# A recurrent attention and a gated network in one planned kernel: decay factors in PSUM, in-place weight conversion, a fourth group buffer, product diagonals for the early groups, and a second DMA queue

## The chip, the cores and the metric

One core of one Trainium2 chip. The metric is the device time of one execution in microseconds, the median of three runs.

## The reference

Two stages, one after the other. The first is a linear recurrence per batch and head (4 batches, 8 heads, 768 tokens, head size 48); the second a gated network on the joined heads (384 columns, 1024 hidden).

```python
for t in range(S):
    cur = einsum('bhd,bhe->bhde', u * k[t], v[t])
    y[t] = einsum('bhd,bhde->bhe', r[t], state + cur)
    state = w * state + einsum('bhd,bhe->bhde', k[t], v[t])

h = maximum(x @ w_in, 0)                      # x: y with its heads joined
conv = sum(conv_w[k] * h shifted by k-1 tokens for k in 0..2)
out = (h * sigmoid(conv)) @ w_out
```

## The kernel before

**Recurrence.** 64 tokens form a chunk, two chunks a group of 128 tokens, six groups a batch; 24 groups in all. Eight heads are four pairs, one head of a pair on partitions 0 to 47, the other on 64 to 111. `load(g)` brings a group into one of `NBUF` buffers: `KR` (k and r with the head dimension on partitions) and `TOK` (k, r and v with tokens on partitions). `prep(g)` scales KR by the decay factors `TKR` (powers of w and their inverses) on VectorE, and TOK's k by `TH`. It also makes the diagonal of the score matrix: r times k, times u, summed over the head dimension (`QQ`), and spread along a diagonal (`SC`, from `eye` and QQ). `visit(g, av, su)` is TensorE's work for a group: `su` makes the next group's scores (`SP`) and state sums (`UP`), `av` this group's output (`AV`). After it, VectorE copies the masked scores into SC (`msk`), the states are updated (`M` decays, `SA` adds; tiles `MM` and `SS`), and `AV` is split into a high and a low part in `XT`. Six small move-copies (SBUF to SBUF DMAs, class `mv`) then bring the fourth pair's rows of XT beside the other three pairs.

**Network.** The tokens of all batches are cut into nine units (the first batch in three of some 256 tokens, the others in two of some 384). For each unit and each of eight hidden blocks, `first(i)` runs nine matmuls into a PSUM bank `HP` (of `NH`), then ReLU, the middle tap (`T1`) on ScalarE, two taps (`T2`, L509) on VectorE into `CV`, the sigmoid into `SG`, the gate product (`GG`, L513) on VectorE, which is the last reader of the HP bank, and a split of the product into two parts in one of 13 `GG` buffers. `second(u, k)` takes three matmuls per hidden block into `PO`; after eight blocks ScalarE copies `PO` to `OS` and a DMA writes it out. "A nine" is nine matmuls of either layer.

**Weights.** They arrive as 64-bit words. `convert` stages a piece in one of `NST` buffers `ST`, makes two 32-bit parts in `CC` (ScalarE) and `TT` (VectorE: a shift, L368, then a combine, L370), and splits the result into a high part (ScalarE cast) and a low part (a subtraction). There are eight pieces of `w_in` and six wider ones of `w_out`.

**Order.** Nothing is scheduled by hand. Every operation is entered in `Plan` with its engines, a duration, and the tiles that it reads and writes. `Plan.order` is a list scheduler: by due times and durations it picks what comes next on each engine, and for operations marked "any" also the engine. It also inserts filler matmuls on `wz` before the first network matmul. The durations are the numbers in `dve`, `pool`, `act` and at each `op`; each engine then keeps the order so found, and the chip's semaphores do the waiting. L272 is the helper `tt` that records all two-input products, so its instructions are told apart by tile. All DMAs are issued from SP (L275).

Of the kernel before, what the change touches and what calls it, by code (L numbers as in the profile page):

```python
# [42 lines left out]
OFF = {"wz": 50.0, "wcz": 60.0}  # L43


class Plan:
# [6 lines left out]
    def __init__(self):  # L53
        self.ops = []
        self.last_w, self.last_r = {}, {}
        self.port = []

    def op(self, eng, dur, rd, wr, fn, cls="", x=0.0, port=False, mode=0):
# [19 lines left out]
        self.port.append(port)  # L78
        return n

    def late(self):
        ops, n = self.ops, len(self.ops)
        late = [1e6] * n
        t = T0
        for i, (dur, x, *_) in enumerate(ops):
            if "pe" in dur and x:
                late[i] = t
                t += dur["pe"]
        for i in reversed(range(n)):
            for j in ops[i][2]:  # L90
                d, x = ops[j][:2]
                m = min(d.values()) + LAT if "sp" not in d else d["sp"] + x + 1.5
                late[j] = min(late[j], late[i] - m)
        return [t - OFF.get(o[4], 0.0) for t, o in zip(late, ops)]

    def order(self):
# [19 lines left out]
        mode = 0  # L116
        todo = n
        while todo:
            best = None
            for e in self.ENG:  # L120
                av, f = avail[e], free[e]
                if e == "pool":
                    c = []
                    for i in av:
                        if len(ops[i][0]) > 1:
                            s = max(free["dve"], ready[i])
                            bl = sum(ops[k][0]["dve"] for k in avail["dve"] if late[k] < late[i] and ready[k] <= s)
                            if max(f, ready[i]) + ops[i][0]["pool"] > s + bl + ops[i][0]["dve"] + PB:
                                continue
                        c.append(i)  # L130
                    av = c
# [53 lines left out]
            elif e == "sp":  # L185
# [3 lines left out]
                lanes.append(done)  # L189
                free[e] = max(free[e], lanes.pop(0))  # L190
# [23 lines left out]
def rwkv_ffn_kernel(tc, krd, krt, vt, wd, ut, w_in, conv_w, w_out, out):  # L214
# [4 lines left out]
    with ExitStack() as ctx:  # L219
# [18 lines left out]
        OS = sb([128, U], F32, "OS", 2)  # L238
        ST = sb([128, 1024], I32, "ST", NST)
        CC, TT = sb([128, 512], F32, "CC", NST), sb([128, 512], I32, "TT", NST)  # L240
# [5 lines left out]
        DN, PW = sb([112, NP, C], F32, "DN"), sb([112, NP, 96], F32, "PW")  # L246
        TKR = sb([112, 2, NP, C], F32, "TKR")
        TK, TR = TKR[:, 0], TKR[:, 1]
        TH = sb([128, NP, D], F32, "TH")
        wi = [sb([128, 3, DF], F32R, f"wi{i}") for i in range(2)]  # L250
# [16 lines left out]

        def tt(eng, n, rd, wr, cls="", psum=0, **kw):
            d = {"dve": dve(n, psum=psum), "pool": pool(n)}
# [4 lines left out]
        def dma(rd, wr, dst, src, dur=0.5, x=0.1, cls=""):  # L274
            op("sp", dur, rd, wr, lambda e: SP.dma_start(dst, src), cls, x)  # L275
# [5 lines left out]
        def warm(e):  # L281
            for _ in range(NW):
                PE.matmul(PO, wz[:, :128], wz, start=True, stop=True)
        op("dve", 0.274, [], ["wz"], lambda e: V.memset(wz, 0.0))
        op("pe", 0.2134 * NW, ["wz"], ["PO"], warm, "warm", 512 * NW)
# [5 lines left out]
        for i, k in enumerate(KR):  # L291
            op("dve", 0.5, [], [n for n in kr(i) if n[2] == 0], lambda e, k=k: V.memset(k[32:64], 0.0), "KRz")

        def load(g):
# [3 lines left out]
            dma([], [("tK", i), ("tR", i)], TOK[i][:, 0:2], krt[g], 0.45, 1.05, "ldT")  # L298
            for x in range(2):
                xs = slice(x * C, (x + 1) * C)  # L300
                dma([], [("tV", i, x)], TOK[i][xs, 2], vt[g, xs, x], 0.45, 0.3, "ldV")

        load(0)
        dma([], ["uu"], uu, ut, 0.45, 0.4, "ldU")
# [50 lines left out]

        ncv = [0]

        def convert(srcs, n, dst, view, keys, cls):
            i = ncv[0] % NST
            ncv[0] += 1  # L360
            st, cc, t = ST[i][:, :2 * n], CC[i][:, :n], TT[i][:, :n]
            s2 = st.rearrange("q (n two) -> q n two", two=2)
            sk = [("ST", i, k) for k in range(len(srcs))]
            for k, (to, src) in zip(sk, srcs):
                dma([], [k], to(st), src, 0.45, n / 352.0 / len(srcs), "wdma")
            op("act", act(n, 1), sk, [("CC", i)], lambda e: A.activation(
                cc, s2[:, :, 1].bitcast(F32), AF.Prelu, scale=2.0 ** -111, alpha=2.0 ** 32))
            op("dve", dve(n, 2) + 0.1, sk, [("TT", i)], lambda e: V.tensor_scalar(  # L368
                out=t, in0=s2[:, :, 0], scalar1=29, scalar2=None, op0=ALU.logical_shift_right), port=True)
            op("dve", dve(n) + 0.06, [("CC", i)], [("TT", i)], lambda e: V.scalar_tensor_tensor(  # L370
                out=t, in0=cc.bitcast(I32), scalar=3, in1=t, op0=ALU.logical_shift_left, op1=ALU.bitwise_or), port=True)
            tf = view(t.bitcast(F32))
            if len(dst) == 1:
                op("act", act(n, 1), [("TT", i)], keys, lambda e: A.activation(dst[0], tf, AF.Copy, scale=1.0 / WS))
                return
            op("act", act(n, 1), [("TT", i)], [keys[0]], lambda e: A.copy(dst[0], tf), cls + "h")
# [17 lines left out]
        def prep(g):  # L394
# [3 lines left out]
            tkr = TKR.rearrange("q a p t -> q (a p) t").unsqueeze(2).broadcast_to([112, 2 * NP, 2, C])  # L398
            if g < 2:
                for h, n in ((0, "KK"), (1, "RR")):  # L400
                    hs = slice(4 * h, 4 * h + 4)
                    tt("dve", 512, ["TK1", "TK2"] if h == 0 else ["TR1", "TR2"], [k for k in kr(i) if k[0] == n], "KR", out=kr_[:, hs], in0=kr_[:, hs], in1=tkr[:, hs], op=ALU.mult)
            else:
                tt("dve", 1024, ["TK1", "TK2", "TR1", "TR2"], kr(i), "KR", out=kr_, in0=kr_, in1=tkr, op=ALU.mult)
            tt("any", 384, [("tK", i)], [("tR", i)], "KRT", out=r_t, in0=r_t, in1=k_t, op=ALU.mult)
            tt("any", 384, ["TH"], [("tK", i)], "KS", out=k_t, in0=k_t, in1=TH.unsqueeze(2).broadcast_to([128, NP, 2, D]), op=ALU.mult)
            tt("any", 384, ["uu"], [("tR", i)], "KRU", out=r_t, in0=r_t, in1=uu.unsqueeze(2).broadcast_to([128, NP, 2, D]), op=ALU.mult)
# [3 lines left out]
            tt("any", 512, [("QQ", g % 2), "eye"], [("SC", g % 2)], "dg", out=SC[g % 2].rearrange("q p c t -> q (p c) t"),  # L411
               in0=eye.unsqueeze(1).broadcast_to([128, 2 * NP, C]), in1=q.unsqueeze(2).broadcast_to([128, 2 * NP, C]), op=ALU.mult)
# [6 lines left out]
        def visit(g, av, su):  # L419
# [9 lines left out]
            if su:  # L429
                rd += kr(j) + [("tK", j), ("tV", j, 0), ("tV", j, 1)]  # L430
                wr += ["SUs", "SUu"]

            def mm(e):
                for c in range(2):
                    for p in range(NP):
# [4 lines left out]
                        for x in range(2):  # L440
                            if su:
                                PE.matmul(SP_[xs[x], p, c], KK[j][rows[x], p, t], RR[j][rows[x], p, t], start=True, stop=True)  # L442
# [206 lines left out]
```

## Time and profile before

| | |
|---|---|
| median of 3 runs | 331.6 us (330.52 to 337.47) |
| profiled execution | 332.88 us, span 331.2 us |
| busy: TensorE, VectorE | 296.4 us (90%), 265.3 us (80%) |
| busy: ScalarE, GpSimd | 168.9 us (51%), 185.5 us (56%) |
| mean granted TensorE clock | 0.948 |
| DMA | 37.78 MB, 114 GB/s on average |

The profile names PE (TensorE matmul), PEld (its weight loads), DVE (VectorE), ACT (ScalarE), POOL (GpSimd) and SP (the engine that issues the DMAs). A group of instructions reads: line, engine, operation, output<-inputs, shapes, count | busy us, mean ns | idle time of the engine just before them and what ended it. A row of the chain of waits reads: start us, duration us, what. "SPq" is SP issuing a DMA.

### The profile page before, as it was taken

The page shows a single profiled execution, that of the slowest core. Times are in us where ns is not written, and L with a number is a line of the kernel's source. Part 1 is how long each engine was busy: PE and PEld are TensorE (multiplying, and loading weights), DVE is VectorE, ACT ScalarE, POOL GpSimd, SP SyncE. Part 2 cuts the span into 40 slices and gives each one's busy share as a digit, 9 for nine tenths or more (in the row PEclk, how much of TensorE's full clock was granted, in tenths as well). Part 3 has the DMA queues.
Part 4 walks back from the last instruction along what each step waited for, and adds up shares of the span by engine and source line. Part 5 has one row for each costly group of instructions (what it writes and reads, how often), then busy time and mean ns, then how long its engine had stood idle before and what let it go on. Part 6 is the DMA issues. An engine that isn't in the chain of part 4 may idle for free.

```text
span 331.2 us, 10563 instructions
## 1 busy us (share of the span) xinstructions
PE 296.4 (90%) x4371; PEld 277.0 (84%) x4371; DVE 265.3 (80%) x439; ACT 168.9 (51%) x380; POOL 185.5 (56%) x201
## 2 busy tenths in 40 slices
PE   6888668795979968998699999999999999999995
PEld 1677657694969967998699999999998999999995
DVE  7897779897988967997597879998999986556630
ACT  2222475664554464376354653676464756567631
POOL 4657668694956844546956746894477632131000
PEclk9797786789899997999799999999999999999999
DMA  6956775745344353455336425443474111000011
GB/s 177 251 160 185 208 226 157 180 132 132 97 115 114 109 149 90 91 131 139 88 101 173 117 81 150 132 113 81 103 179 107 35 34 41 12 26 25 26 48 49
DMA packets 25952, 37.78 MB, mean 114 GB/s; under 512 B 5168, under 2 KB 19504, under 8 KB 25904
## 3 DMA queue, kind: packets, MB, share of 16 engines
q1 hardware_dynamic: 25904, 37.11, 42.1%
q8 instruction: 34, 0.56, 0.7%
q14 instruction: 14, 0.11, 0.1%
HBM read 30.01 MB, written 4.72 MB: 105 GB/s over the span
## 4 chain that ended last, share of the span: by engine, by line
PE 50%; DVE 20%; DMA 10%; issue 6%; POOL 6%; ACT 5%; SPq 2%; DVEq 0%; ACTq 0%; POOLq 0%
PE HP L500 20%; PE PO L532 19%; DMA ST<-in_w_out_dram 6%; DVE CV L509 4%; DVE KR L272 3%; PE SP L442 3%; PE HP L532 3%; POOL TOK L272 2%; DVE GG L272 2%; PE AV L452 2%; POOL GG L272 2%; SPq L275 2%; PE AV L445 2%; DMA TOK<-in_krt_dram 2%; DVE TT L370 1%
## 5 line engine op out<-in xcount | busy, mean ns | idle before, releaser
L500 PE MATMUL HP<-XT,wi 128*128 128x384 f32 (+4 forms) x648 | 123.3, 339 | 15.6 <-DVE SG L513 10.2
L500 PEld LDWEIGHTS HP<-XT,wi 128*128 128x128 f32 x648 | 110.9, 204 | 18.7 <-DVE SG L513 11.8
L532 PE MATMUL PO<-GG,wo 128*128 128x382 f32 (+4 forms) x600 | 110.7, 327 | 8.6 <-POOL GG L272 2.9
L532 PEld LDWEIGHTS PO<-GG,wo 128*128 128x128 f32 x600 | 97.7, 194 | 12.3 <-POOL GG L272 3.7
L509 DVE SCALAR_TENSOR_TENSOR CV<-HP,cw,CV 128x382 f32<-128x382 f32 (+4 forms) x144 | 77.2, 565 | 12.5 <-ACT CV L506 11.9
L272 POOL TENSOR_TENSOR GG<-SG,GG 128x382 fp32r<-128x382 f32 (+4 forms) x48 | 49.6, 1044 | 32.6 <-ACT GG L515 29.9
L505 ACT ACTIVATE HP<-HP 128x384 f32<-128x384 f32 (+4 forms) x72 | 31.8, 441 | 57.3 <-PE HP L500 56.9
L513 DVE TENSOR_TENSOR SG<-HP,SG 128x382 f32<-128x382 f32 (+4 forms) x72 | 35.6, 507 | 19.2 <-ACT SG L512 18.7
L512 ACT ACTIVATE SG<-CV 128x382 f32<-128x382 f32 (+4 forms) x72 | 34.4, 487 | 27.9 <-DVE CV L509 21.6
L442 PE MATMUL SP<-KR 48*64 48x64 f32 x768 | 46.7, 233 | 0.8 <-DVE SC L457 0.4
L452 PE MATMUL AV<-SC,TOK 64*48 64x64 f32 x768 | 47.1, 222 | 0.0
L272 POOL TENSOR_TENSOR TOK<-TOK 128x384 f32<-128x384 f32 x23 | 24.4, 1062 | 37.4 <-DMA TOK<-in_krt_dram 36.7
L445 PE MATMUL AV<-KR,SS 48*48 48x64 f32 x704 | 44.2, 223 | 0.4 <-DVE XT L272 0.2
L442 PEld LDWEIGHTS SP<-KR 48*64 48x64 f32 x768 | 39.2, 138 | 6.0 <-issue 2.2
L272 DVE TENSOR_TENSOR KR<-KR,TKR 112x1024 f32<-112x1024 f32 (+1 forms) x26 | 44.0, 1698 | 0.1
L449 PE MATMUL UP<-TOK 64*48 64x48 f32 x704 | 41.2, 209 | 1.2 <-DVE SS L272 1.2
L506 ACT ACTIVATE CV<-HP,cw 128x382 f32<-128x382 f32 (+4 forms) x72 | 39.1, 544 | 1.0
L515 ACT CAST GG<-SG 128x382 fp32r<-128x382 f32 (+4 forms) x72 | 33.3, 473 | 8.7 <-DVE SG L513 8.5
L272 POOL TENSOR_TENSOR MM<-SS,PW 112x192 f32<-112x192 f32 x38 | 27.1, 712 | 19.0 <-DVE SS L272 18.4
L452 PEld LDWEIGHTS AV<-SC,TOK 64*48 64x48 f32 x768 | 36.1, 124 | 0.0
L449 PEld LDWEIGHTS UP<-TOK 64*48 64x48 f32 x704 | 34.2, 126 | 1.7 <-DVE SS L272 1.4
L445 PEld LDWEIGHTS AV<-KR,SS 48*48 48x48 f32 x704 | 33.1, 124 | 0.9 <-DVE XT L272 0.6
(61 smaller groups left out, 318.1 us busy)
## 6 DMA issues: line engine op xcount, KB each, us to landing
TOK<-in_krt_dram SPq DMA_DIRECT2D x24, 384.0 KB, 3.8
KR<-in_krd_dram SPq DMA_DIRECT2D x48, 192.0 KB, 3.8
TOK<-in_vt_dram SPq DMA_DIRECT2D x48, 96.0 KB, 3.6
ST<-in_w_in_dram SPq DMA_DIRECT2D x8, 384.0 KB, 3.4
ST<-in_w_out_dram SPq DMA_DIRECT2D x6, 512.0 KB, 5.0
XT<-XT SPq DMA_DIRECT2D x144, 16.0 KB, 2.2
out_dram<-OS SPq DMA_DIRECT2D x9, 193.0 KB, 2.1
out_dram<-OS SPq DMA_DIRECT2D x9, 191.0 KB, 2.6
```

Source lines behind the costliest of these rows:

```text
L272: op(eng, d, rd, wr, lambda e: e.tensor_tensor(**kw), cls, port=not psum)
L442: PE.matmul(SP_[xs[x], p, c], KK[j][rows[x], p, t], RR[j][rows[x], p, t], start=True, stop=True)
L445: PE.matmul(outs[x], state(2 * g + c)[rows[x], p], RR[i][rows[x], p, t], start=True, stop=False)
L449: PE.matmul(UP[rows[x], n:n + D], TOK[j][xs[x], 0, p, c], TOK[j][xs[x], 2, p, c], start=True, stop=True)
L452: PE.matmul(outs[x], TOK[i][xs[x], 2, p, c], SC[g % 2][xs[x], p, c], start=first and c == 0, stop=True)
L500: PE.matmul(hp, wi[a][:, j, fs], X[:, x, j, t], start=(j == 0 and k == 0), stop=(j == 2 and k == 2))
L506: op("act", act(n, 0, 1), [H_, "cw"], [("T", ti)], lambda e: A.activation(t1, hp[:, 1:n + 1], AF.Copy, scale=cw[:, 3 * f + 1:3 * f + 2]), ...
L509: op("dve", dve(n, psum=1) + 0.02, [H_, "cw"], [("T", ti)], lambda e, k=k: V.scalar_tensor_tensor(out=t1, in0=hp[:, k:n + k], scalar=cw[:, ...
L512: op("act", act(n, 1), [("T", ti)], [("SG", ti)], lambda e: A.activation(sg, t1, AF.Sigmoid))
L513: op("dve", dve(n), [H_], [("SG", ti)], lambda e: V.tensor_tensor(out=sg, in0=hp[:, 1:n + 1], in1=sg, op=ALU.mult), "GG")
L515: op("act", act(n, 1), [("SG", ti)], [("GH", gi)], lambda e: A.copy(gh, sg))
L532: PE.matmul(po[:, :n], wo[a][:, f, ms], g2[x], start=(f == 0 and j == 0), stop=(f == NF - 1 and j == 2))
```

## The change

- The decay factors `TKR` move from SBUF to a PSUM bank; one HP bank is given up for it (`NH` 4 to 3).
- `convert` works in place: shift and combine write into the staging buffer itself; ScalarE's part goes into `PO` for the narrow pieces and into the staging buffer for the wide ones. `CC` and `TT` disappear, and there are three staging buffers.
- Four group buffers instead of three; one `OS` buffer instead of two.
- For groups 0 to 8 (`DQ` = 9) the diagonal comes from TensorE: `KP` = k times r with the head dimension on partitions (both scaled), and one-column matmuls of KP with `uw` (u times w) into free columns of `UP`; ScalarE copies the eight columns to QQ. The r part of TOK is not loaded for these groups. Later groups keep the old way.
- The two first groups' visits are split into an `av` and a `su` visit.
- DMAs can be issued from ACT: the first group's tokens, all output writes, and for groups 0 to 2 the move-copies where the scheduler wants it. Diagonal and decay products may go to ACT, in pieces.
- The buffers' zero rows of KR are written by ACT, but for the first. `DN` shares a tile with `CV`.
- New durations throughout, and new rules in `Plan.order` for VectorE and GpSimd: a VectorE operation with two SBUF inputs waits for a running GpSimd operation and the other way round, where durations were stretched before.

```diff
-NBUF = 3
+NBUF = 4
-NH = 4
+NH = 3
-NST = 2
+NST = 3
+DQ = 9
+GQ = 3
+SPLIT = 2
...
-                if e == "dve" and self.port[i]:
-                    d += SLOWER * max(0.0, min(d, free["pool"] - s))
-                if e == "pool" and free["dve"] > s:
-                    d *= SHARED
+                d += begin(e, i) - s
+                if e == "dve" and self.port[i]:
+                    lock = s + d
...
-        TKR = sb([112, 2, NP, C], F32, "TKR")
+        TKR = pst.tile([128, 2, NP, C], F32, name="TKR")
...
-            st, cc, t = ST[i][:, :2 * n], CC[i][:, :n], TT[i][:, :n]
+            st = ST[i][:, :2 * n]
             s2 = st.rearrange("q (n two) -> q n two", two=2)
+            lo, hi = s2[:, :, 0], s2[:, :, 1]
+            cc, key = (PO[:, :n], "PO") if n != 512 else (hi.bitcast(F32), ("CC", i))
...
-                out=t, in0=s2[:, :, 0], scalar1=29, scalar2=None, op0=ALU.logical_shift_right), port=True)
+                out=lo, in0=lo, scalar1=29, scalar2=None, op0=ALU.logical_shift_right))
...
-            tt("any", 384, [("tK", i)], [("tR", i)], "KRT", out=r_t, in0=r_t, in1=k_t, op=ALU.mult)
+            if g >= DQ:
+                tt("any", 384, [("tK", i)], [("tR", i)], "KRT", out=r_t, in0=r_t, in1=k_t, op=ALU.mult)
             tt("any", 384, ["TH"], [("tK", i)], "KS", ...)
+            if g < DQ:
+                tt("any", 512, kr(i), ["KP"], "KP", out=KP..., in0=KK[i], in1=RR[i], op=ALU.mult)
+                return
...
                                 PE.matmul(SP_[xs[x], p, c], KK[j][rows[x], p, t], RR[j][rows[x], p, t], start=True, stop=True)
+                                if g + 1 < DQ:
+                                    n = 2 * NP * D + 2 * p + c
+                                    PE.matmul(UP[xs[x], n:n + 1], KP[rows[x], p, c], uw[rows[x], p:p + 1], start=True, stop=True)
...
+                if gn < DQ:
+                    op("act", 0.2, ["SUu"], [("QQ", k)], lambda e: A.copy(QQ[k], UP[:, 2 * NP * D:2 * NP * D + 2 * NP]), "q")
+                    diag(gn)
```

What the scheduler makes of it at three places. First, VectorE around the preparation of an early group, while the wide weight pieces are converted. Before (`QQ` reduces, L368 and L370 shift and combine, `KR` scales):

```order
L409 TENSOR_REDUCE QQ_75<-TOK_65 128x8
L272 TENSOR_TENSOR SS_70<-MM_73,UP 112x192
L272 TENSOR_TENSOR wo_119<-TT_104,wo_118 128x4x128
L272 TENSOR_TENSOR KR_63<-KR_63,TKR 112x1024
L457 COPY_PREDICATED SC_67<-mask,SP 128x512
L272 TENSOR_TENSOR SS_71<-MM_74,UP 112x192
L368 TENSOR_SCALAR TT_104<-ST_100 128x512
```

and with the change, the same kind of place (L291 is the helper, L402 and L404 shift and combine, L570 the taps, L574 the gate product):

```order
L404 SCALAR_TENSOR_TENSOR ST_102<-ST_102 128x512
L574 TENSOR_TENSOR SG_84<-HP_123,SG_84 128x256
L570 SCALAR_TENSOR_TENSOR CV_82<-HP_124,cw,CV_82 128x256
L291 TENSOR_TENSOR wo_117<-ST_102,wo_116 128x4x128
L291 TENSOR_TENSOR KR_63<-KR_63,TKR 112x1024
L574 TENSOR_TENSOR SG_85<-HP_124,SG_85 128x256
L512 COPY_PREDICATED SC_70<-mask,SP 128x512
```

The reduction is gone, and the wide pieces' conversion now stands among the taps and gate products of a unit of 256 tokens. Second, VectorE at the start of the first long unit. Before, with four HP banks:

```order
L509 SCALAR_TENSOR_TENSOR CV_79<-HP_124,cw,CV_79 128x382
L509 SCALAR_TENSOR_TENSOR CV_80<-HP_125,cw,CV_80 128x382
L409 TENSOR_REDUCE QQ_76<-TOK_66 128x8
L513 TENSOR_TENSOR SG_82<-HP_124,SG_82 128x382
L509 SCALAR_TENSOR_TENSOR CV_80<-HP_125,cw,CV_80 128x382
L272 TENSOR_TENSOR KR_61<-KR_61,TKR 112x1024
L513 TENSOR_TENSOR SG_83<-HP_125,SG_83 128x382
```

and with three:

```order
L570 SCALAR_TENSOR_TENSOR CV_82<-HP_124,cw,CV_82 128x382
L448 TENSOR_REDUCE QQ_78<-TOK_66 128x8
L574 TENSOR_TENSOR SG_84<-HP_123,SG_84 128x382
L570 SCALAR_TENSOR_TENSOR CV_82<-HP_124,cw,CV_82 128x382
L570 SCALAR_TENSOR_TENSOR CV_83<-HP_125,cw,CV_83 128x382
L574 TENSOR_TENSOR SG_85<-HP_124,SG_85 128x382
L570 SCALAR_TENSOR_TENSOR CV_83<-HP_125,cw,CV_83 128x382
```

The gate product of one bank now follows within two or three operations of its own last tap. Third, the DMA queue ahead of the first network matmul, with the move-copies (`XT<-XT`) of the first two groups. Before, all on SP:

```order
L275 DMA XT_77<-XT_77 16x2x128
L275 DMA ST_101<-in_w_in_dram 128x768
L275 DMA XT_77<-XT_77 16x2x128
L275 DMA ST_100<-in_w_in_dram 128x768
L275 DMA XT_77<-XT_77 16x2x128 x4
L275 DMA KR_62<-in_krd_dram 48x1024
L275 DMA XT_77<-XT_77 16x2x128 x2
L275 DMA ST_101<-in_w_in_dram 128x768
```

With the change, on SP:

```order
L295 DMA ST_103<-in_w_in_dram 128x768
L295 DMA XT_79<-XT_79 16x2x128 x3
L295 DMA TOK_65<-in_vt_dram 64x384
L295 DMA KR_62<-in_krd_dram 48x1024 x2
L295 DMA TOK_66<-in_krt_dram 128x384
L295 DMA XT_79<-XT_79 16x2x128 x3
```

and on ACT:

```order
L295 DMA XT_79<-XT_79 16x2x128
L400 ACTIVATE PO<-ST_101 128x384
L295 DMA XT_79<-XT_79 16x2x128 x2
L540 CAST XT_79<-AV 112x4x128
L400 ACTIVATE PO<-ST_102 128x384
L411 CAST wi_114<-ST_101 128x3x128
L295 DMA XT_79<-XT_79 16x2x128 x2
L400 ACTIVATE PO<-ST_103 128x384
L295 DMA XT_79<-XT_79 16x2x128
```

Of the twelve move-copies six stand on each queue; on ACT they stand among the conversion's activations.

More of the change, by code (lines that the diff above doesn't have):

```diff
@@ L91, in late @@
                 d, x = ops[j][:2]
-                m = min(d.values()) + LAT if "sp" not in d else d["sp"] + x + 1.5
+                m = min(d.values()) + (x + 1.5 if self.moves[j] else LAT)
                 late[j] = min(late[j], late[i] - m)
@@ L116, in order, with begin, takes @@
         mode = 0
+        lock = 0.0
         todo = n
+        def begin(e, i):
+            t = max(free[e], ready[i])
+            if e == "dve" and self.port[i] and free["pool"] > t:
+                t = free["pool"]
+                t += max([ops[k][0]["pool"] for k in avail["pool"] if k != i and ready[k] <= t and len(ops[k][0]) == 1], default=0.0)
+            if e == "pool":
+                t = max(t, lock)
+            return t
+        def takes(e, i):
+            end = begin(e, i) + ops[i][0][e]
+            for v in ops[i][0]:
+                if v != e:
+                    t = max(free[v], ready[i])
+                    bl = sum(ops[k][0][v] for k in avail[v] if late[k] < late[i] and ready[k] <= t and len(ops[k][0]) == 1)
+                    if end > begin(v, i) + bl + ops[i][0][v] + (PB if v == "dve" else 0.0):
+                        return False
+            return True
         while todo:
@@ L121, in order @@
                 av, f = avail[e], free[e]
[L122 to L131, printed above, removed]
+                av = [i for i in av if len(ops[i][0]) == 1 or takes(e, i)]
                 if not av:
@@ L354, in rwkv_ffn_kernel, with uq @@
         op("act", 0.4, ["SUs"], ["TH"], lambda e: A.copy(TH, SP_.rearrange("q p c t -> q (p c t)")[:, 0:NP * D].rearrange("q (p d) -> q p d", p=NP)))
+        def uq(e):
+            for p in range(NP):
+                for x in range(2):
+                    PE.matmul(UP[64 * x:64 * x + D, 400 + p:401 + p], uu[64 * x:64 * x + 1, p], ident[64 * x:64 * x + 1, 0:1], start=True, stop=True)
+        op("pe", 0.3, ["uu", "ident"], ["SUu"], uq, "uq", 10, mode=1)
+        op("dve", 0.15, ["SUu", ("wc", 0), ("wc", 1)], ["uw"], lambda e: V.tensor_tensor(out=uw, in0=UP[0:112, 400:400 + NP], in1=wc, op=ALU.mult), "uw")
         ncv = [0]
@@ L410, in prep, with diag, spread @@
                 out=q, in_=r_t.rearrange("q p c d -> q (p c) d"), axis=AX.X, op=ALU.add), "QQ")
-            tt("any", 512, [("QQ", g % 2), "eye"], [("SC", g % 2)], "dg", out=SC[g % 2].rearrange("q p c t -> q (p c) t"),
-               in0=eye.unsqueeze(1).broadcast_to([128, 2 * NP, C]), in1=q.unsqueeze(2).broadcast_to([128, 2 * NP, C]), op=ALU.mult)
+            diag(g)
+        def diag(g):
+            q = QQ[g % 2]
+            sc = SC[g % 2].rearrange("q p c t -> q (p c) t")
+            def spread(e):
+                if e is not A:
+                    return e.tensor_tensor(out=sc, in0=eye.unsqueeze(1).broadcast_to([128, 2 * NP, C]), in1=q.unsqueeze(2).broadcast_to([128, 2 * NP, C]), op=ALU.mult)
+                for n in range(2 * NP):
+                    A.activation(sc[:, n], eye, AF.Copy, scale=q[:, n:n + 1])
+            op("any", {"pool": 1.0, "dve": dve(512), "act": 2 * NP * act(C, 0.155)}, [("QQ", g % 2), "eye"], [("SC", g % 2)], spread, "dg", port=True)
         w64 = PW[:, :, 64:65].broadcast_to([112, NP, D])
@@ L469, in visit, with decay @@
                         m = MM[c]
-                        tt("any", 192, [ka, "PW2"], [("M", c)], "M", out=m, in0=a, in1=w64, op=ALU.mult)
+                        def decay(e, m=m, a=a):
+                            if e is not A:
+                                return e.tensor_tensor(out=m, in0=a, in1=w64, op=ALU.mult)
+                            for p in range(NP):
+                                A.activation(m[:, p], a[:, p], AF.Copy, scale=PW[:, p, 64:65])
+                        op("any", {"pool": pool(192), "dve": dve(192), "act": NP * act(48, 0.155)}, [ka, "PW2"], [("M", c)], decay, "M", port=True)
                         tt("dve", 192, [("M", c), "SUu"], [kb], "SA", 1, out=b, in0=m, in1=u_, op=ALU.add)
@@ L558, in visits @@
                     prep(g + 1)
-                visit(g, True, g + 1 < NG)
+                if g < SPLIT:
+                    visit(g, True, False)
+                    visit(g, False, True)
+                else:
+                    visit(g, True, g + 1 < NG)
                 if g + NBUF < NG:
@@ L584, in rwkv_ffn_kernel @@
                 if i < 0:
-                    PE.matmul(PO[:, :FN], wz[:, :128], wz[:, :FN], start=True, stop=True)
+                    PE.matmul(HP[NH - 1][:, :FN], wz[:, :128], wz[:, :FN], start=True, stop=True)
                 else:
```

105 lines of the change are left out of this document (59 added, 46 removed).

## The prediction, made before the changed kernel ran

> **What bounds the kernel now.** I read the page first (busy shares, slices), then the stages by windows, then the groups of VectorE (DVE) in the first stage, then the waits and the chain. The page says that TensorE (PE) is the long pole, and where it is not:
>
> ```profile
> span 331.2 us, 10563 instructions
> PE 296.4 (90%) x4371; PEld 277.0 (84%) x4371; DVE 265.3 (80%) x439; ACT 168.9 (51%) x380; POOL 185.5 (56%) x201
> PE   6888668795979968998699999999999999999995
> DVE  7897779897988967997597879998999986556630
> PEclk9797786789899997999799999999999999999999
> ```
>
> The profiled execution took 332.88 us, 1.7 more than its span; the median of the three runs is 331.6, 1.3 below that execution. From the middle on, PE is full in every slice. In the first third it has gaps, its clock drops, and DVE is as full as PE. The stages, cut at the first matmul of the recurrence, at the first one of the network, at the third of the nine token units, and at the last recurrence step (columns: time, PE, weight loads, DVE, ACT, POOL busy, clock, DMA share, GB/s):
>
> ```profile
> 0.00:14.20 14.20, 9.70 (x48) 4.83 (x48) 11.84 (x23) 3.56 (x8) 7.84 (x22) 0.88 0.84 219
> 14.20:36.70 22.50, 17.76 (x390) 15.02 (x389) 17.91 (x28) 5.62 (x13) 15.02 (x16) 0.92 0.61 167
> 36.70:108.00 71.30, 58.63 (x910) 54.06 (x910) 62.18 (x105) 39.51 (x101) 50.69 (x51) 0.86 0.56 153
> 108.00:260.00 152.00, 142.82 (x2382) 136.92 (x2380) 131.62 (x215) 81.59 (x179) 98.80 (x100) 0.98 0.46 117
> 260.00:327.60 67.60, 67.53 (x650) 66.21 (x648) 41.72 (x74) 38.17 (x79) 13.13 (x14) 1.00 0.09 30
> ```
>
> PE busy counts half-clock time and fillers as work, so I price PE's real work at full clock from the chain of waits: nine matmuls of the first layer, nine of the second, for long and short units, and one recurrence visit (it fills the gap from 198.47 to 200.43):
>
> ```profile
> 110.92 1.09 PE HP L500 x9
> ...
> 187.34 1.60 PE HP L500 x9
> 188.94 1.58 PE PO L532 x9
> ...
> 196.90 1.57 PE HP L500 x9
> 200.43 1.27 PE PO L532 x6
> ```
>
> There are 24 short and 48 long nines in each layer and 24 visits: 24 x 1.09 + 48 x 1.60 + 24 x 1.09 + 48 x 1.58 + 24 x 1.96 = 252. So 331 - 252 = 79 us of the span is not PE work. Up to 108 us some 20 short nines of the first layer, 13 of the second and 7 visits are done, 20 x 1.09 + 13 x 1.09 + 7 x 1.96 = 50 us of work: 58 us are lost there (14 of them before the first visit). After 108 there are 202 us of work in 223: 21 lost, 3.6 of them the tail. **The first 108 us are the place.** There DVE is busy 11.8 + 17.9 + 62.2 = 92 us. Its groups up to 108 us:
>
> ```profile
> L272 DVE TENSOR_TENSOR KR<-KR,TKR 112x1024 f32<-112x1024 f32 x7 | 12.2, 1740 | 0.0
> L370 DVE SCALAR_TENSOR_TENSOR TT<-CC,TT 128x512 int32<-128x512 int32 x6 | 8.2, 1360 | 0.0
> L368 DVE TENSOR_SCALAR TT<-ST 128x384 int32<-128x384 int32 x8 | 6.4, 807 | 3.5 <-DMA ST<-in_w_in_dram 3.5
> L368 DVE TENSOR_SCALAR TT<-ST 128x512 int32<-128x512 int32 x6 | 5.9, 988 | 0.0
> L272 DVE TENSOR_TENSOR SC<-eye,QQ 128x512 f32<-128x512 f32 x2 | 4.7, 2371 | 0.0
> L272 DVE TENSOR_TENSOR XT<-AV,XT 112x512 fp32r<-112x512 f32 x7 | 4.7, 676 | 0.4 <-ACT XT L479 0.4
> L272 DVE TENSOR_TENSOR SS<-MM,UP 112x192 f32<-112x192 f32 x13 | 4.4, 342 | 1.5 <-PE UP L449 1.5
> L409 DVE TENSOR_REDUCE QQ<-TOK 128x8 f32<-128x384 f32 x8 | 4.4, 545 | 0.0
> L292 DVE MEMSET KR<- 32x1024 f32 x3 | 2.7, 912 | 0.7 <-issue 0.7
> ```
>
> Second, the weights: the chain of waits before 80 us runs through the staging buffers' transfers, and move-copies (L275 on SP's queue) sit ahead of one of them:
>
> ```profile
> 33.28 0.59 SPq L275
> ...
> 35.89 3.57 DMA ST<-in_w_in_dram
> 40.14 6.15 DMA ST<-in_w_out_dram
> ...
> 55.44 5.87 DMA ST<-in_w_out_dram
> ...
> 73.26 6.85 DMA ST<-in_w_out_dram
> ```
>
> **The change, part by part, up to 108 us.**
>
> *Decay factors in PSUM.* The same instruction on the same shape takes very different times:
>
> ```profile
> 105.36 1.21 DVE L272 TENSOR_TENSOR KR<-KR,TKR 112x1024 f32<-112x1024 f32 x1
> 230.53 4.47 DVE L272 TENSOR_TENSOR KR<-KR,TKR 112x1024 f32<-112x1024 f32 x1
> ```
>
> 4.47 - 1.21 is a wait inside the instruction, with POOL working beside it. With a PSUM operand there is no row for 1024 elements; from the two rows that have one, XT (512 in 0.68) and SS (192 in 0.34), 0.34 us per 320 elements gives 0.68 + 512 x 0.34 / 320 = 1.22, and neither of them shows the wait. So 7 x (1.74 - 1.22) = 3.6 us go. The Trainium skill, page "SBUF — State Buffer", section "Who interferes with whom", states that VectorE and GpSimd share one pair of SBUF ports, held for the whole instruction, which an op with two SBUF inputs needs; by that rule, too, the factors' move ends the wait, and the two rows agree.
>
> *Early diagonals.* For groups 0 to 8 the reduction QQ goes from DVE (8 x 0.545 = 4.4), and the two wide SC products (4.7) go to POOL or ACT; two KP products come to DVE (512 elements, an XT row: 2 x 0.68 = 1.4). Two POOL products per group become one. Two memsets go to ACT: 1.8. Sum for DVE: 4.4 + 4.7 + 1.8 - 1.4 = 9.5. PE gains 16 one-column products per group. The nearest row is the first visit, at half clock: 64 matmul records from
>
> ```profile
> 14.27 0.26 PE SP L442 x4
> ...
> 16.06 0.11 PE UP L449 x4
> ```
>
> 1.9 us, so 30 ns a record and 15 at full clock; 32 new records (each f32 product shows as two) are 0.5 us a visit if nothing hides them and 0 if they slip between the others. Nine visits: 0 to 4.5, and while DVE is the bound PE has room; I take 2. The diagonal now waits for the visit's own sum (copy, diagonal, mask), some 2 us more latency per group; network matmuls stand between the visits and cover that, except in the first three visits.
>
> *In-place conversion, three staging buffers.* Shift and combine have waits of the same kind: the 384-wide shift took 0.36 alone,
>
> ```profile
> 39.56 0.36 DVE L368 TENSOR_SCALAR TT<-ST 128x384 int32<-128x384 int32 x1 [1.20 <-DMA ST<-in_w_in_dram]
> ```
>
> against a mean of 0.81; 8 x 0.45 = 3.6. I put the wide combine and the wide shift alone at 0.68 and 0.48 (the 384-wide times by length, the combine like XT): 6 x 0.68 + 6 x 0.51 = 7.1. Together 10.7 us of waiting. Only the 384-wide combine gets a PSUM operand; the rest loses its waits only as far as POOL has less to do. I credit 5, with bounds 0 and 10.7. The Trainium skill, page "VectorE: DVE Perf Modes", section "Mode 2×_2P", says that a one-source op from SBUF to SBUF uses both read ports; 384 words in 0.36 us, faster than the XT row's rate, agrees, and by that rule the shift's share of the credit, some 2.5, does not come, whatever the planner now assumes; the sum below would then be 2.5 x 0.85 = 2 us higher. The third buffer lets a transfer (3.6 to 6.9 us in the chain) run beside two conversions.
>
> *Two queues, four group buffers.* Half of the move-copies of groups 0 to 2 leave SP's queue (0.6 us each in the chain), so the first network matmul, which needs twelve of them, comes 12 x 0.6 / 2 = some 4 us sooner. POOL no longer waits for tokens. Cost: a group is fetched earlier, in competition with the weights. ACT gets the output DMAs, the decay products in four pieces and some diagonals; it is half idle (51%) and covers them, if nothing urgent queues behind them. The Trainium skill, page "Trainium Kernel Development and Optimization", section "Key Constraints", says that several issuing queues save issue time only, as all share the DMA engines; that is why no bandwidth is credited here.
>
> *Sum up to 108 us.* DVE loses 3.6 + 9.5 + 5 = 18 of 92 us. It was busy 85% of the stage; 18 x 0.85 = 15 us is what I let the stage shrink, to 93. PE (50 + 2) and DMA allow it: 14.2 x 219 + 22.5 x 167 + 71.3 x 153 = 17.8 MB, at the 219 GB/s of the first row 81 us. The earlier start and the third buffer are not added: they are what lets DVE be fed.
>
> *After 108 us.* Here the KR product still waits:
>
> ```profile
> L272 DVE TENSOR_TENSOR KR<-KR,TKR 112x1024 f32<-112x1024 f32 x14 | 27.2, 1943 | 0.0
> ```
>
> 14 x (1.94 - 1.22) = 10 us of DVE, which has 132 busy of 152; of the 17 us that PE loses before the tail I give back 5. The price is one HP bank less: the first layer's nine must wait until its third predecessor is multiplied by the gate (L513), not its fourth. With four banks the wait is already there in the first 108 us:
>
> ```profile
> PEld HP L500 <- DVE SG L513: 8.5, 6, 2.5
> ```
>
> The new DVE order multiplies by the gate right behind the taps, so I take +2, bounds 0 and the rival below. Sum: 331.2 - 15 - 5 + 2 = 313 (PE's 2 lie inside the first stage). With 1.7 outside the span and 1.3 for the median: 313 to 314. **I predict 313.**
>
> **Rivals.**
>
> *Three banks bind (slower).* In the old order, the nine of 201.70 (it ends at 203.28) is multiplied by the gate as the first of two products that start at 216.26, but its third successor starts at 212.84:
>
> ```profile
> 201.70 1.58 PE HP L500 x9
> ...
> 212.84 1.58 PE HP L500 x9
> 216.26 1.00 DVE L513 TENSOR_TENSOR SG<-HP,SG 128x382 f32<-128x382 f32 x2
> ```
>
> That product ends near 216.8, so three banks would have cost 4 us there. If DVE falls behind so at half of the 14 visits of this stage, that is 28 us against gains of 20: 339. It decides as soon as the time from a nine's end to its gate product passes 212.84 - 203.28 = 9.6 us. For it: 216.8 - 203.3 = 13.5 us in the example. Against: the new order, and 10 us less on DVE. Chance 0.08.
>
> *The weights still set the pace.* If the early transfers, with one more group in front of them, land when they did (last one issued at 73.26), the second layer starts no sooner; then only the start (4) and the late 5 count, less 2: 331.2 - 7 + 0.4 = 325. For it: the chain. Against: three buffers, 192 of 960 KB less per early group (by the tiles' shapes). Chance 0.17.
>
> *PE full from early on.* If the stage falls to its DMA bound of 81 and the later loss halves by 8: 331 - 27 - 8 = 296 to 300. Chance 0.10. That the move to PSUM does not do what it says, and the wait stays: 313 + 3.6 x 0.85 + 5 = 321, inside the range.
>
> **How the numbers follow.** Forecast (305 to 320) 0.65, the others 0.17, 0.10, 0.08. The range leaves out the slow rival and the lowest end: 299 to 327. 2% is about what this kernel's measurement tells from no change, 325: faster holds the forecast, the fast rival and a third of the weights' rival, 0.65 + 0.10 + 0.06 = 0.81; the same the rest of that rival, 0.11; slower 0.08.
>
> **What would show it.** The KR group at about 1.2 us, no wider spread; no QQ group for nine groups; third unit's taps (258 columns) near 93 us instead of 108; first network matmul near 32; PE's wait for L513 not over 10 us in all; ACT's gaps not on the chain. Wrong would be: that wait at 20 us or more, the w_out transfers still on the chain past 70 us, or ACT's DMA issues ahead of ReLUs on the chain.

## The result, and the profile after

The changed kernel took 320.11 us (median of four runs, 318.13 to 322.23) against 332.97 us for the kernel before on the same chip (330.52 to 337.47). The ratio is 0.9638, with an interval of 0.9534 to 0.9743: faster. A ratio, here and below, is made from undisturbed runs alone, so it can differ a little from the quotient of two medians. The profiled execution took 322.23 us, 1.7 more than its span.

The page after, in the lines that were shown of before:

```profile
span 320.5 us, 11145 instructions
PE 293.5 (92%) x4653; PEld 275.9 (86%) x4653; DVE 252.3 (79%) x447; ACT 196.2 (61%) x489; POOL 135.6 (42%) x152
PE   6887875879899999999999999999998999999895
DVE  5778779889999879999979878989778776566520
PEclk9799975999999999999999999999999999999999
```

PE has no slice under 80% from the tenth (72 us) on until the last, where before it had holes up to the twentieth. GpSimd lost 50 us of work, VectorE only 13. The windows tell where the time came from. Before (time; PE, weight loads, DVE, ACT, POOL busy; clock; DMA share; GB/s):

```profile
0.00:96.00 96.00, 74.71 (x1156) 63.27 (x1156) 82.35 (x139) 43.70 (x108) 66.97 (x80) 0.86 0.63 169
96.00:160.00 64.00, 55.51 (x1024) 52.42 (x1024) 54.56 (x96) 32.41 (x78) 38.53 (x42) 0.97 0.46 117
```

and after:

```profile
0.00:96.00 96.00, 77.35 (x1529) 68.05 (x1530) 80.60 (x142) 56.82 (x153) 51.88 (x68) 0.93 0.64 168
96.00:160.00 64.00, 62.37 (x1102) 59.65 (x1101) 58.31 (x111) 45.71 (x126) 35.52 (x37) 1.00 0.47 129
```

Up to 96 us VectorE, whose relief was to shorten this stage, is busy 1.75 us less, not 18. Between 96 and 160 us PE is busy 62.4 us instead of 55.5, and at full clock. The same is seen in the start of three units' first nine on PE's timeline (third unit: 260 columns; fourth: 384; fifth: 388; in brackets PE's idle time and what ended it). Before:

```profile
96.41 1.82 PE L500 MATMUL HP<-XT,wi 128*128 128x260 f32 x9 [1.43 <-DVE CV L509]
126.67 3.22 PE L500 MATMUL HP<-XT,wi 128*128 128x384 f32 x9 [1.40 <-DMA XT<-XT]
160.09 2.89 PE L500 MATMUL HP<-XT,wi 128*128 128x388 f32 x9 [2.95 <-DVE SG L513]
```

and after:

```profile
95.41 1.35 PE L561 MATMUL HP<-XT,wi 128*128 128x260 f32 x9
121.17 3.41 PE L561 MATMUL HP<-XT,wi 128*128 128x384 f32 x18
148.64 1.76 PE L561 MATMUL HP<-XT,wi 128*128 128x388 f32 x9
```

1.0 us is gained at the third unit, 5.5 at the fourth, 11.4 at the fifth, and 10.7 at the end of the span. So nearly the whole gain is made between 96 and 160 us; the first 96 us bring 1.0 us, and the last 160 nothing. These are the starts in one execution of each kernel.

**Where VectorE's relief went.** Its groups up to 96 us that changed most. Before:

```profile
L272 DVE TENSOR_TENSOR KR<-KR,TKR 112x1024 f32<-112x1024 f32 x6 | 11.0, 1828 | 0.0
L272 DVE TENSOR_TENSOR wi<-TT,wi 128x384 fp32r<-128x384 f32 x2 | 1.2, 596 | 0.0
```

and after:

```profile
L291 DVE TENSOR_TENSOR KR<-KR,TKR 112x1024 f32<-112x1024 f32 x8 | 9.7, 1212 | 0.0
L402 DVE TENSOR_SCALAR ST<-ST 128x512 int32<-128x512 int32 x6 | 7.3, 1223 | 0.0
L402 DVE TENSOR_SCALAR ST<-ST 128x384 int32<-128x384 int32 x8 | 4.1, 512 | 0.0
L291 DVE TENSOR_TENSOR wi<-ST,wi 128x384 fp32r<-128x384 f32 x3 | 4.9, 1619 | 1.1 <-ACT wi L411 1.1
```

The KR product takes 1.21 us, as forecast, but eight groups are prepared in this time instead of six. The wide shift (0.988 us before) takes 1.22, a weight subtraction 1.62 instead of 0.60, a TH product 1.72 instead of 1.21: some operations with SBUF operands alone take longer now. Not all do: the narrow shift takes 0.51 instead of 0.81, and the wide combine 1.37, as before (1.36). GpSimd works 15 us less in this time (66.97 to 51.88).

**The hole that closed.** PE ran out of work before the fourth unit's first nine, because the move-copies (XT<-XT) of the group that it needs were late. SP's queue before, from its timeline (start, duration, DMA):

```profile
116.43 4.46 SPq L275 DMA_DIRECT2D XT<-XT  x6
120.98 0.99 SPq L275 DMA_DIRECT2D KR<-in_krd_dram  x2
...
122.69 3.78 SPq L275 DMA_DIRECT2D XT<-XT  x6
```

and after:

```profile
112.47 2.03 SPq L295 DMA_DIRECT2D KR<-in_krd_dram  x2
...
115.21 3.78 SPq L295 DMA_DIRECT2D XT<-XT  x6
```

The copies are all issued by 126.47 us before and by 118.99 after. Before, PE was idle for 2.9 us, waiting for GpSimd's part of a gate product, and for another 1.4 until the copies landed; then it ran that nine at half clock (0.52 granted), in 3.23 us. A second hole before the fifth unit ends with a gate product (the 2.95 us above). The chain ahead of it goes back to a load that came late: GpSimd's products of a group's tokens wait for it, GpSimd's part of a gate product stands behind them, and the taps and the gate product follow late.

```profile
143.75 5.54 DMA TOK<-in_krt_dram
149.36 1.02 POOL TOK L272
...
159.50 0.44 DVE SG L513
160.09 2.89 PE HP L500 x9
```

After, neither hole is there, and the clock stays at 1.00.

### The profile page after: what moved, and what is told of

The parts are those of the page before. It is cut to its first block, busy times and chain, and to the rows that moved or that the text cites. A ratio compares the mean times of both kernels' runs of the same rounds, so it can differ in the third digit from the quotient of the medians.

```text
span 320.5 us, 11145 instructions
## 1 busy us (share of the span) xinstructions
PE 293.5 (92%) x4653; PEld 275.9 (86%) x4653; DVE 252.3 (79%) x447; ACT 196.2 (61%) x489; POOL 135.6 (42%) x152
## 4 chain that ended last, share of the span: by engine, by line
PE 42%; DVE 24%; DMA 13%; ACT 11%; issue 4%; SPq 3%; POOL 1%; ACTq 1%; DVEq 0%
PE PO L593 15%; PE HP L561 14%; DVE CV L570 7%; DMA KR<-in_krd_dram 6%; DMA TOK<-in_krt_dram 3%; PE SP L491 3%; SPq L295 3%; DVE KR L291 3%; PE HP L593 3%; PE AV L504 2%; DVE ST L404 2%; DVE SG L574 2%; DVE ST L402 2%; ACT SG L573 2%; PE UP L501 2%
## 5 line engine op out<-in xcount | busy, mean ns | idle before, releaser
L561 PE MATMUL HP<-XT,wi 128*128 128x384 f32 (+4 forms) x648 | 115.8, 325 | 5.0 <-DVE SG L574 5.0
L561 PEld LDWEIGHTS HP<-XT,wi 128*128 128x128 f32 x648 | 105.1, 192 | 6.2 <-DVE SG L574 5.6
L570 DVE SCALAR_TENSOR_TENSOR CV<-HP,cw,CV 128x382 f32<-128x382 f32 (+4 forms) x144 | 80.0, 568 | 10.0 <-ACT CV L567 8.5
L291 POOL TENSOR_TENSOR GG<-SG,GG 128x386 fp32r<-128x386 f32 (+4 forms) x43 | 39.3, 915 | 106.8 <-ACT GG L576 99.3
L491 PE MATMUL SP<-KR 48*64 48x64 f32 x768 | 53.4, 231 | 1.7 <-DVE SC L512 1.7
L491 PEld LDWEIGHTS SP<-KR 48*64 48x64 f32 x768 | 44.0, 136 | 6.5 <-issue 2.4
L574 DVE TENSOR_TENSOR SG<-HP,SG 128x382 f32<-128x382 f32 (+4 forms) x72 | 36.5, 509 | 13.6 <-ACT SG L573 12.6
L501 PE MATMUL UP<-TOK 64*48 64x48 f32 x704 | 47.1, 209 | 0.0
L501 PEld LDWEIGHTS UP<-TOK 64*48 64x48 f32 x704 | 37.8, 124 | 0.0
L291 DVE TENSOR_TENSOR KR<-KR,TKR 112x1024 f32<-112x1024 f32 (+1 forms) x26 | 29.2, 1130 | 4.8 <-DMA KR<-in_krd_dram 3.9
L458 POOL TENSOR_TENSOR SC<-eye,QQ 128x512 f32<-128x512 f32 x22 | 24.2, 1099 | 18.3 <-PE AV L504 10.5
L291 DVE TENSOR_TENSOR GG<-SG,GG 128x382 fp32r<-128x382 f32 (+4 forms) x29 | 19.9, 687 | 7.5 <-ACT GG L576 7.1
```

What stands on the lines that cost most here:

```text
L291: op(eng, d, rd, wr, lambda e: e.tensor_tensor(**kw), cls, port=not psum)
L501: PE.matmul(UP[rows[x], n:n + D], TOK[j][xs[x], 0, p, c], TOK[j][xs[x], 2, p, c], start=True, stop=True)
L561: PE.matmul(hp, wi[a][:, j, fs], X[:, x, j, t], start=(j == 0 and k == 0), stop=(j == 2 and k == 2))
L570: op("dve", dve(n) + 0.06, [H_, "cw"], [("T", ti)], lambda e, k=k: V.scalar_tensor_tensor(out=t1, in0=hp[:, k:n + k], scalar=cw[:, 3 * f + ...
L574: op("dve", dve(n), [H_], [("SG", ti)], lambda e: V.tensor_tensor(out=sg, in0=hp[:, 1:n + 1], in1=sg, op=ALU.mult), "GG")
```

## The experiments

Three theories stood after the traces. Theory 1: VectorE's relief (the KR product in PSUM above all) carries the gain after 96 us. Theory 2: a group's loads no longer come late, through the fourth buffer or the second queue. Theory 3: the scheduler's order carries it. Where an edit lets the schedule be made anew, the order changes with the part, so that such a run tells of both.

**One part undone.** First the decay factors, with every engine's order kept. To make room in SBUF two early tiles share later ones, and one small copy is added.

```diff
-        TKR = pst.tile([128, 2, NP, C], F32, name="TKR")
+        TKR = sb([112, 2, NP, C], F32, "TKR")
...
```

> The changed kernel with the decay factors back in SBUF, every engine's order kept as it is. Theory 1 (the time gained after 96 us is VectorE's relief): the KR product goes back to some 1.9 us each, 22 x 0.7 = 15 us of VectorE, most of it after 96 us, where VectorE paces TensorE; 8 to 12 us slower, 328 to 332. Theory 2 (the gain after 96 us is that a group's loads no longer come late): the KR product is slower by the same 0.7 us, but TensorE has work in hand; 0 to 3 us slower, 320 to 323.

Measured: 324.49 us, ratio 0.9736 (0.968 to 0.9792), against 0.9638 of the whole change. The KR group of this kernel:

```profile
L292 DVE TENSOR_TENSOR KR<-KR,TKR 112x1024 f32<-112x1024 f32 x22 | 32.9, 1494 | 2.1 <-DMA KR<-in_krd_dram 2.1
```

1.49 us instead of 1.21: 22 x 0.28 = 6 us of VectorE come back, where I expected 15, probably because GpSimd is less often in the way (it is busy 142.7 us here, 185.5 before the change). Some 3 us of time (0.9736 less 0.9638) go with it, though the intervals overlap. Theory 1 expected 8 to 12, theory 2 up to 3; the median of 324.49 us lies in neither range, nearer to theory 2's.

Three group buffers:

```diff
-NBUF = 4
+NBUF = 3
```

> The changed kernel with three group buffers instead of four (the schedule is made anew). Theory 2 (loads no longer late): each load starts one group later, GpSimd waits for tokens as before the change (36.7 us over the run then, 10.2 with it), and 5 to 10 us of the 11 gained after 96 us go: 325 to 330. Theory 1 (VectorE's relief): under 2 us, 319 to 322.

Measured: 317.82 us, 0.9539 (0.9492 to 0.9587), no slower than the whole change. All DMAs on SP:

```diff
-GQ = 3
+GQ = 0
...
-        load(0, "act")
+        load(0)
...
-                dma([("OS", q)], ..., o, 0.55, n / 700.0, "out", "act")
+                dma([("OS", q)], ..., o, 0.55, n / 700.0, "out")
```

> The changed kernel with all DMAs issued from SP again (the schedule is made anew). Theory 2 (loads no longer late): output writes at the head of SP's queue wait for ScalarE's copy out of PO, and the loads behind them come late, as before the change (SP waited 46.4 us for these copies): 4 to 10 us slower, 324 to 330; the first network matmul 2 to 4 us later. Theory 1 (VectorE's relief): only the first network matmul moves, 1 to 3 us, 321 to 323.

Measured: 321.32 us, 0.9627 (0.9559 to 0.9696), as the whole change. Both answers speak against theory 2. With three buffers GpSimd waited 8.4 us for tokens over the run, with four 10.2, before the change 36.7: in the new order it is not the fourth buffer that brings the loads in time. No one-column products:

```diff
-DQ = 9
+DQ = 0
```

> The changed kernel with all diagonals made the old way (reduction on VectorE, no one-column products; the schedule is made anew). If the products save what the prediction gave them (9.5 us of VectorE in the first stage, less 1.8 for the memsets that stay on ScalarE, at 0.85, less 2 of TensorE): 4 to 7 us slower, 324 to 327. If they cost TensorE about what they save VectorE (nine visits went from 2.0 to 2.8 us, 7 us in all): within 2 us, 318 to 322.

Measured: 318.97 us, 0.9556 (0.9491 to 0.962). The products save nothing that shows.

**Several parts undone, or one done alone.** The changed kernel again, beside the next three:

> The changed kernel itself, as the measure for the other three on this chip. All theories: 0.964 of the kernel before, 318 to 322.

Measured: 322.77 us, 0.9638 (0.9479 to 0.9796). Four parts undone at once (the edits above for buffers, queue and products, and):

```diff
-SPLIT = 2
+SPLIT = 0
```

> The changed kernel with four of its parts undone at once: three group buffers, one DMA queue, no product diagonals, no split visits (schedule made anew). Each of the first three alone moved the time by under 1% or made it faster. Theory 3 (the order and the PSUM move carry the gain, these parts do nothing together either): 317 to 322. Theory 2 in a weaker form (each covers for the others: buffers, queue and fewer loads all bring the tokens in time, and one of them is enough): 326 to 331, with GpSimd waiting 30 us or more for tokens.

Measured: 323.41 us, 0.9761 (0.9602 to 0.992). The time lies between the two ranges, and the interval is wide enough for both, so the time alone does not decide. GpSimd waited 21.9 us for tokens, 36.7 before the change, 10.2 with it, under the 30 that a hidden theory 2 asked for. Nor does the sum of these waits follow the time: it is 12.0 us with the scheduler's durations alone (329.94 us, below) and 18.9 in the last experiment (319.94 us). A single late load can still matter, as at the second hole of the kernel before.

The kernel before with the scheduler's rules and durations alone. No buffer, bank, queue or operation differs from before:

```diff
-            return 0.14 + 0.06 * psum + n / 960.0 / two
+            return 0.065 + n / 960.0
...
-            return 0.2 + n * 0.0021
+            return 0.02 + n * 0.00247
...
-                    d += SLOWER * max(0.0, min(d, free["pool"] - s))
+                    lock = s + d
...
```

> The kernel before, with nothing of the change but the scheduler's rules and durations. Theory 3a (the new order carries the gain: the gate product behind its own taps, GpSimd's work not started ahead of VectorE's): 318 to 325. Theory 3b (the freed VectorE time carries it, the order nothing): 330 to 335.

Measured: 322.68 us, 0.9733 (0.9655 to 0.9811). What the scheduler decides, the order and for operations marked "any" the engine, makes the kernel 2.7% faster by itself, at least 1.9% by the interval. (VectorE has 454 instructions instead of 439, GpSimd 186 instead of 201: 15 operations changed engine.) This is called the order alone below. And the PSUM move alone:

```diff
-NH = 4
+NH = 3
...
-        TKR = sb([112, 2, NP, C], F32, "TKR")
+        TKR = pst.tile([128, 2, NP, C], F32, name="TKR")
...
```

> The kernel before with the decay factors in PSUM and three HP banks, nothing else (old scheduler rules and durations). Theory 1 (VectorE's relief carries the gain): the KR product takes 1.22 us, 22 x 0.7 = 15 us of VectorE go: 321 to 326. Theory 3a (the order carries it): three banks in the old order make the gate product's lateness bind, 333 to 340. In between, 328 to 332, if the relief and the lost bank cancel.

Measured: 331.61 us, 0.9995 (0.995 to 1.004): nothing. Its page, and its KR group:

```profile
span 331.2 us, 10543 instructions
PE 293.6 (89%) x4369; PEld 275.0 (83%) x4369; DVE 245.0 (74%) x445; ACT 172.0 (52%) x380; POOL 168.0 (51%) x195
L272 DVE TENSOR_TENSOR KR<-KR,TKR 112x1024 f32<-112x1024 f32 x22 | 26.7, 1212 | 5.4 <-DMA KR<-in_krd_dram 5.4
```

VectorE is relieved of 20 us (265.3 to 245.0): 6.0 in the first 108 us (91.9 to 86.0), where the forecast gave this part 3.6, and 14 after them, where it gave 10. The span is the same to a tenth. TensorE's starts show what became of it. The first network matmul before:

```profile
36.68 4.94 PE L500 MATMUL HP<-XT,wi 128*128 128x256 f32 x27 [2.49 <-DMA XT<-XT]
```

and with the PSUM move alone the first network matmul, the third unit, then SP's copies and the fourth unit:

```profile
39.15 5.08 PE L500 MATMUL HP<-XT,wi 128*128 128x256 f32 x27 [5.80 <-DMA XT<-XT]
100.62 2.30 PE L500 MATMUL HP<-XT,wi 128*128 128x260 f32 x9 [1.68 <-DVE CV L509]
127.02 3.78 SPq L275 DMA_DIRECT2D XT<-XT  x6
131.01 4.95 PE L500 MATMUL HP<-XT,wi 128*128 128x384 f32 x18 [2.89 <-DMA XT<-XT]
```

With less work on VectorE the first network matmul is 2.5 us later than in the kernel before, the third unit 4.2, and the copies and the nine at the hole 4.3. The fifth unit, at 161.09 us, is 1.0 us later, and at the end nothing is left of the difference. PE waited 11.1 us for move-copies over this run, 3.9 before the change. The schedule of this kernel, too, was made anew for three banks, so it does not tell the relief, the lost bank and the order apart; it shows that 20 us less on VectorE need not shorten the kernel. With the new order alone everything comes earlier (timelines of the kernel with the scheduler's rules and durations):

```profile
32.85 0.98 PE L514 MATMUL HP<-XT,wi 128*128 128x256 f32 x3 [2.40 <-DMA XT<-XT]
92.89 1.60 PE L514 MATMUL HP<-XT,wi 128*128 128x260 f32 x9 [0.99 <-DVE GG L286]
117.32 3.78 SPq L289 DMA_DIRECT2D XT<-XT  x6
122.28 3.31 PE L514 MATMUL HP<-XT,wi 128*128 128x384 f32 x18
```

3.8 us are gained at the first network matmul, 3.5 at the third unit, 4.4 at the fourth, 9.1 at the fifth (151.04 us) and 10.3 at the end of the span. So this kernel closes both holes too, but a third of its gain lies ahead of the third unit, where the changed kernel has 1.0 us. Part of the reason why the copies at the hole come earlier is that they need the visit of their group, and the visit stands earlier on PE. The chain before, and then of this kernel (SP is the first tile of a visit, PO the second layer):

```profile
113.81 2.13 PE PO L532 x18
115.94 0.20 PE SP L442
...
124.61 1.93 DMA XT<-XT
126.67 3.23 PE HP L500 x9
```

```profile
109.48 0.70 PE PO L546 x6
110.19 0.20 PE SP L456
```

Before, two nines of the second layer stood just ahead of the visit, now six matmuls do, and the visit starts at 110.2 instead of 115.9 us; 3.5 of these 5.7 us were gained already at the third unit. SP's queue is the other part: from 107.8 to 126.5 us it issued almost without pause before, six copies and a group's loads in turn, and the new order begins the first of these copies at 101.7 us.

**Rules or durations, and the sum.** The new rules with the old durations:

> The kernel before with the scheduler's new rules for VectorE and GpSimd alone, the old durations. Rules and durations together, nothing else, gave 0.973. Theory 3c (it is the rules: an operation that would wait inside itself for GpSimd is put elsewhere): 0.970 to 0.980, 322 to 326, and the KR product's spread shrinks as with both (longest 2.6 us instead of 4.5). Theory 3d (it is the durations): 0.993 to 1.005, 330 to 334.

Measured: 333.65 us, 1.0028 (0.9989 to 1.0066). The new durations with the old rules:

> The kernel before with the scheduler's new durations alone, the old rules. Theory 3d (it is the durations: DMA issues at 0.55 to 0.59 us, GpSimd's operations dearer, VectorE's and ScalarE's cheaper): 0.970 to 0.980, 322 to 326. Theory 3c (it is the rules): 0.993 to 1.005, 330 to 334.

Measured: 329.94 us, 0.9896 (0.9844 to 0.9949). Neither theory holds as stated: the durations give 1%, the rules nothing, and both together 2.7%. The windows show it from 96 to 160 us, for the rules,

```profile
96.00:160.00 64.00, 56.73 (x1024) 52.39 (x1024) 50.09 (x88) 32.14 (x77) 42.70 (x44) 0.97 0.45 118
```

for the durations,

```profile
96.00:160.00 64.00, 59.76 (x1152) 56.94 (x1150) 55.38 (x102) 35.05 (x84) 45.12 (x46) 0.97 0.48 124
```

and for both:

```profile
96.00:160.00 64.00, 61.51 (x1157) 58.44 (x1156) 58.12 (x103) 37.41 (x87) 46.99 (x48) 0.97 0.52 128
```

PE's busy time there goes 55.5 (before), 56.7, 59.8, 61.5. VectorE's busy time does not explain it: the rules alone relieve it (245.5 us over the whole run, 265.3 before) and gain nothing, though the longest KR product falls from 4.47 to 2.88 us, much as theory 3c expected of them; with both VectorE is busy 256.7 us, and the kernel is faster. Why rules and durations need each other is not settled; the two make different lists on every engine.

Rules, durations and the PSUM move together (the two edits above in one kernel):

> The kernel before with the new rules and durations and the decay factors in PSUM (three HP banks), nothing else. The PSUM move alone gave 0.9995, rules and durations alone 0.973. If the effects only add: 0.973, 322 to 324. If VectorE's relief is worth something once the order lets TensorE run full (moving the factors back into SBUF cost the changed kernel 1%): 0.960 to 0.966, 319 to 322, as the whole change, and the other parts together are worth nothing.

Measured: 327.28 us, 0.9813 (0.9769 to 0.9858): slower than without the PSUM move, outside both expectations. Its schedule was made anew for three banks, so the move, the lost bank and the order are not told apart by it.

Last, the two edits that alone had seemed to help, in one kernel:

```diff
-NBUF = 4
+NBUF = 3
-DQ = 9
+DQ = 0
```

> The changed kernel with three group buffers and without product diagonals, both at once (schedule made anew); alone they gave 0.954 and 0.956 against 0.964 of the whole change. If each saves what it seems to (three buffers an earlier first stage, no products 0.8 us a visit for nine visits): 0.944 to 0.950, 315 to 317. If the two were only other orders of the same worth: 0.955 to 0.968, 318 to 322.

Measured: 319.94 us, 0.9604 (0.9556 to 0.9652). The two effects do not add. It reaches the third unit 6.8 us sooner than the changed kernel, and the fourth 2.7:

```profile
88.62 2.44 PE L561 MATMUL HP<-XT,wi 128*128 128x260 f32 x18
118.45 3.42 PE L561 MATMUL HP<-XT,wi 128*128 128x384 f32 x18
```

The time came out the same: what an order gains early is lost again later. Every kernel whose schedule was made anew with the new rules and durations lies between 0.954 and 0.981, whatever parts it holds; differences of 1% among them are no evidence for a part. The lowest of them, three buffers with all else of the change, took 317.82 us; it beats the kernel before clearly, and the changed kernel by no more than this spread.

No run adds or undoes by itself the in-place conversion with its third staging buffer, or ScalarE's share of the diagonal and decay products. Whether they bring part of the 1% between the order alone (0.9733) and the whole change (0.9638) is not shown; it is no more than the spread between orders.

## Why the prediction was right or wrong

The kernel became faster, as forecast, and 320 us lies in the range of 299 to 327, 7 us above the 313 of the sum. That the total fits is luck, since its parts do not: the sum took 15 us from the time up to the third unit and 3 from the rest; on TensorE 1.0 us was gained up to that unit and 9.7 behind it.

- **The failed step: "18 of 92 us ... is what I let the stage shrink, to 93".** Up to 96 us VectorE lost 1.75 us and the third unit started 1.0 us earlier. The cut at 108 us, "at the third of the nine token units", is that unit's first taps on VectorE; TensorE had begun the unit at 96.41. Counted to these taps VectorE lost 8 us (91.9 to 84.0), not 18. The single prices were right in part (the KR product, the reductions gone); the 5 us for the conversion were not: shifts and combines took 25.5 us before and 24.0 after. The rest of the relief was filled by longer waits in other operations, by two groups prepared sooner and by work taken from GpSimd. The deeper error is the assumption under it, that an engine busy 85% of a stage sets its length. The PSUM move alone freed 20 us of VectorE, 6.0 of them in the first 108 us, and its third unit started 4.2 us later. The rules alone freed 20 us, 4.3 of them in that stage (91.9 to 87.6), and their third unit started 0.1 us earlier. Neither moved the time.
- **Where the gain came from was not in the sum.** I gave the stage after 108 us 3 us (5 less 2). From the third unit on 10 us were gained, at two places where PE ran dry at a unit's start. The rows were there before: a chain through SP's issues from 121 us to the copies' landing, and a nine of twice its length behind it; at the second place a load of tokens that GpSimd waited for. I priced durations and never asked whether the work order, which the change also makes anew, was the limit. The order alone gave a ratio of 0.9733, the whole change 0.9638. How far its rules, its durations and single moves in it make this gain stays open.
- **The KR product at 1.22 us:** measured 1.212, all 22 alike. Right, and worth some 3 us of time at a fixed order, with overlapping intervals.
- **No QQ for nine groups:** right; with the products left out the kernel was no slower.
- **The one-column products, "0 to 0.5 us a visit":** too low. A visit with them and one without, as windows:

```profile
101.37:104.19 2.82, 2.82 (x162) 2.77 (x161) 2.82 (x7) 1.21 (x4) 1.86 (x2) 1.00 0.31 84
110.01:112.04 2.03, 2.03 (x130) 1.95 (x129) 1.87 (x4) 1.48 (x5) 0.38 (x1) 1.00 0.29 89
```

  0.79 us for 32 records, 25 ns each instead of 15; nine visits cost PE 7 us, not 2.
- **First network matmul near 32 us:** it came at 35.5 us, 1.2 sooner than before, although half of the twelve copies stood on ACT's queue. The last copies were issued 3 us sooner (by 32.8 us instead of 35.8), but those of the second group took 3.2 to 3.4 us from issue to landing instead of 1.9 to 3.1, and the split that they need ended no sooner (at 30.5 us, 30.4 before).
- **Third unit's taps near 93 instead of 108:** measured 99.35 instead of 107.97. VectorE did reach them 8.6 us sooner, while PE's matmuls for them started only 1.0 us sooner; the marker spoke of the engine that did not bind.
- **Three banks, "+2":** PE's waits for the gate product in the changed kernel were

```profile
PE HP L561 <- DVE SG L574: 5.0, 2, 4.4
```

  in all, half of the 10.2 before and under the 10 that I gave as the mark, and the rival with 339 us fell. The wait did not grow by 2, it shrank by 5; no run has four banks in the new order, so the price of the bank itself is not shown.
- **The weights:** the last w_out transfer is issued at 68.13 us instead of 73.26, the last one on the chain at 58.80, and still the third unit starts only 1.0 us sooner. Neither the rival that held them to be the pace nor my answer to it told what binds those 96 us. Three buffers and no products together shortened them by 6.8 us, to no gain at the end; what binds them is open.

## What to carry to other kernels

Before an engine's relief is counted as time, find the moment at which the bound engine runs dry and name what it waits for there; an average share of 85% names nothing. Where a change also makes a schedule anew, run the new order with the old parts first: here it alone gave most of the gain, and among schedules made anew 1% is noise between orders. And look at what stands ahead of the one long-latency step (here a visit, its copies and their queue): work that could fill the wait belongs behind it.

## What the runs showed of the hardware

A matmul of one column is far from free. In the changed kernel, one line of the page for 64 columns, and one of the groups for one column:

```profile
L491 PE MATMUL SP<-KR 48*64 48x64 f32 x768 | 53.4, 231 | 1.7 <-DVE SC L512 1.7
L494 PE MATMUL UP<-uw,KP 48*64 48x1 f32 x288 | 21.9, 184 | 1.3 <-DVE SS L291 1.3
```

184 ns against 231 from start to end, and 25 ns of PE's time for each in a packed visit. The second thing: TensorE ran slowly behind a wait. In the kernel with the PSUM move alone, 18 matmuls of 384 columns took 4.95 us right behind a wait of 2.89 us, at a granted clock of 0.66; in the changed kernel 18 took 3.41 us at 1.00, so 1.5 us were lost behind the wait. In the kernel before, the nine at the hole took 3.22 us at 0.52; there eight matmuls of the second layer, between its two waits of 2.92 and 1.40 us, still ran at 0.97. That the wait brings the low clock is not shown by a run of its own.
